# Score matmuls of two batches in four quarter tiles and two PSUM banks, with larger strided groups

## The chip, the cores and the metric

The kernel runs on one core of one Trainium2 chip. The metric is the device time of one execution in microseconds. It is one launch; inputs lie in DRAM and the output goes back there.

## The reference

Three blocks in a row over 4 batches of 576 positions: attention with 8 heads of 64, a gated feed-forward block with a spatial matmul over positions, and a block with sine and cosine and a second matmul over positions. The change is in the attention alone:

```python
B, H, S, D = q.shape                      # 4, 8, 576, 64
scores = scale * np.matmul(q, k.transpose(0, 1, 3, 2))
rel = pos[:, None] - pos[None, :]
mask_local = (rel >= 0) & (rel < stride)  # stride = 32, heads 0 to 3
mask_strided = (rel >= 0) & (pos[None, :] % stride == pos[:, None] % stride)  # heads 4 to 7
scores = np.where(masks, scores, -1e9)
attn = np.exp(scores - np.max(scores, axis=-1, keepdims=True))
attn = attn / (np.sum(attn, axis=-1, keepdims=True) + 1e-09)
out = np.matmul(attn, v)
```

## The kernel before

The two later blocks are the main work: for each batch `main_v`, `main_mid` (chunks named `u`, `sp`, `x`, `th` in the profile) and `main_end` (`y`, `c`), all matmuls in f16 with high and low parts. A chunk of main work takes one slot of the pool `ps_m`, three slots of two PSUM banks each (`pm(name)`). Attention of batch 0 runs first, that of batches 1 and 2 (`attention1`) and of batch 3 (`attention`, f16) runs beside the main work of the batch before. In the profile all instructions have line 107, the helper that records them, so one goes by tiles: `sc` scores, `sm` softmax, `st` its maxima and sums, `pT` transposed probabilities, `av` a PSUM bank for transposes and P·V, `xT` the attention's output, which is the next batch's main input.

Heads go in pairs `hp` (0 and 1 local, 2 and 3 strided); `j` is the head in the pair, and head `j` of a pair lies on partitions 64j to 64j + 63 of `q` and `k`, so its matmuls use row half j of the array. Because of the mask a local block of 64 queries needs 96 keys, and a strided block (queries and keys sorted by position modulo 32) 54 queries and 54 keys, of which the tile holds 64. `groups` (line 452) joins blocks to groups: five local ones of 4, 4, 2, 4, 4 blocks and four strided ones of 6, 6, 6, 4. A group is one chain: `gr_scores` (two matmuls a block, one a head, head j's queries on output partitions 64j and up, all in the one bank `sc`, with a mask added by a matmul of the identity), `gr_shift` (VectorE: maximum, subtraction), `gr_exp` (ScalarE), `gr_div` (VectorE: sum, two small ones, product), `gr_turn` (TensorE transposes into `av`, ScalarE copy to `pT`), `gr_px` (P·V: `v` stationary, `pT` moving, head j on output partitions 64j and up; local groups into `av`, strided ones with alternate blocks in `sc` and `av`) and `gr_parts` (ScalarE and VectorE write high and low part of `xT`). `sc` and `av` are one bank each with a single buffer.

`attention1` is a generator: step s emits P·V of group s - 2, scores, maximum, subtraction and exponential of group s, the transposes of s - 1 and the division of s, and gives control back. `others`, called after each piece of main work, takes the next step of batch b when the main matmuls' own clock has reached `ATT_AT[b][0] + n * ATT_AT[b][1]` us (line 57). That is the order in which instructions are handed over. A planner then orders each engine's instructions by its own estimate of when each is ready, gives out the slots of the pools as they come free in that estimate, and sets the semaphores; `not_before` keeps scores behind a main matmul 3 us of the clock earlier. On the chip each engine runs its instructions in the order planned. So a matmul that has to wait holds up all of TensorE behind it.

Of the kernel before, what the change touches and what calls it, by code (L numbers as in the profile page):

```python
# [56 lines left out]
ATT_AT = (None, (2.7, 3.9), (86.0, 5.0), (174.5, 4.6))  # L57
# [12 lines left out]
def kernel(  # L70
# [397 lines left out]
    def load_vl(b, hp, v):  # L468
        src = vl_d[b, hp].rearrange("p n j d -> p n (j d)")
        c = slice(1, VW - 1)  # L470
# [7 lines left out]
    def load_vs(b, v, hps=(2, 3)):  # L478

        src = vs_d[b].rearrange("h p n j d -> p h n (j d)")  # L480
        c = slice(1, VW - 1)
# [3 lines left out]
        for i in range(11):  # L485
            k, end = CB * i, min(CB * i + CB, S)
            o = 0
            while k < end:
# [6 lines left out]
                else:  # L495
                    for u, hp in enumerate(hps):
                        r = 64 * (hp - 2) + o
                        nc.sync.dma_start(v[r:r + m, u, i // 2, c], src[p0:p0 + m, hp - 2, n])
# [3 lines left out]
    mask64 = const.tile([P, 2, 96], BF16, name="mask64")  # L502
    mask54 = const.tile([P, QB], BF16, name="mask54")

    def make_masks():
# [14 lines left out]
        for j in range(2):  # L520
            h = slice(64 * j, 64 * j + 64)
            nc.vector.tensor_copy(mask64[h], a[h, j])
# [57 lines left out]
    def gr_div(g, sm, st):  # L580

        local, blocks = groups[g]
        n, w = len(blocks), 96 if local else QB
        p, sums = sm[:, 0:n * w].rearrange("p (n c) -> p n c", c=w), st[:, 1, 0:n]
        nc.vector.tensor_reduce(out=sums, in_=p, op=ALU.add, axis=mybir.AxisListType.X)
        nc.vector.tensor_scalar(sums, sums, 1e-9, 1.0 / XS, op0=ALU.add, op1=ALU.mult)
        nc.vector.reciprocal(sums, sums)
        nc.vector.tensor_tensor(p, p, sums.unsqueeze(2).broadcast_to([P, n, w]), ALU.mult)

# [35 lines left out]

    def gr_px(b, g, v, pT):


        local, blocks = groups[g]
        banks = (pa("av"),) if local else (pa("sc"), pa("av"))  # L630
        nb = len(banks)
        for i, (hp, blk) in enumerate(blocks):
            r = 64 * (i % 2)
            m = QB if local else min(CB, S - CB * blk)
            for j in range(2):
                c = slice(1 + 64 * j, 65 + 64 * j)
                q = slice(64 * j, 64 * j + m)
                if local:
                    lhs, rhs = v[hp][0:96, blk, c], pT[0:96, i, q]
                else:  # L640
                    lhs, rhs = v[hp][r:r + m, blk // 2, c], pT[r:r + m, i // 2, q]
                nc.tensor.matmul(banks[i % nb][64 * j:64 * j + 64, QB * (i // nb):QB * (i // nb) + m], lhs, rhs,
                                 start=True, stop=True)
        for i in range(nb):
# [662 lines left out]
```

## Time and profile before

| what | value |
|---|---|
| time, median of 3 runs | 500.48 us (500.36 to 502.01) |
| the profiled execution, its span from first to last instruction | 505.4 us |
| instructions | 10756 |
| TensorE busy in the span | 482.8 us |
| VectorE, ScalarE, GpSimd busy | 303.1, 268.1, 73.5 us |
| mean granted clock of TensorE | 0.985 of full speed |

The profiled execution is one of its own, and its span is the time that the profile gives for it. Busy times of an engine are unions: overlapping matmuls count once. In a timeline row the first number is the start, the second the time from the first start to the last end of the instructions merged in the row; in brackets stands the idle time before it and what ended it.

### The profile page before, as it was taken

To read this page: it belongs to the slowest core of one execution; us is meant where nothing else is said; L and a number is where in the kernel's file an instruction comes from. 1 tells how busy PE (TensorE), PEld (TensorE's weight loads), DVE (VectorE), ACT (ScalarE), POOL (GpSimd) and SP (SyncE) were. 2 spreads that over 40 slices of the span, in tenths; PEclk is the share of its full clock that TensorE was granted. 3 is DMA by queue.
4 is the path that set the end of the run, shared out by engine and by line. 5 is a ranking of instruction groups with operands and counts; after the bars stand their busy time and mean duration, and the time that the engine had idled before them with its cause. 6 is when DMAs were issued, how large, how long until landed. Compare 5 with 4: busy or idle time off the path is not lost. (4 is left out here: it accounts for less than half of the span.)

```text
span 505.4 us, 10756 instructions
## 1 busy us (share of the span) xinstructions
PE 482.8 (96%) x4420; PEld 361.0 (71%) x4420; DVE 303.1 (60%) x649; ACT 268.1 (53%) x484; POOL 73.5 (15%) x69
## 2 busy tenths in 40 slices
PE   7789988999899999999999999899999999999997
PEld 5575666766467777777748878677757777777775
DVE  3665899676798545763398678773498121217412
ACT  2555877778975234445684657765772022148302
POOL 2022324320003300021000510021003200210220
PEclk9969999999899999999999999999999999999999
DMA  7967456684671036200076054521090020002602
GB/s 181 266 205 187 143 182 197 251 249 119 167 185 39 1 119 197 73 27 3 2 163 177 17 126 128 120 53 22 7 173 10 0 94 1 1 2 66 122 1 95
DMA packets 71820, 52.72 MB, mean 104 GB/s; under 512 B 50584, under 2 KB 59992, under 8 KB 71770
## 3 DMA queue, kind: packets, MB, share of 16 engines
q1 hardware_dynamic: 71466, 51.42, 37.7%
q8 instruction: 35, 0.57, 0.5%
q10 hardware_dynamic: 304, 0.61, 0.4%
q14 instruction: 15, 0.12, 0.1%
HBM read 35.36 MB, written 4.72 MB: 79 GB/s over the span
## 5 line engine op out<-in xcount | busy, mean ns | idle before, releaser
L107 PE MATMUL y<-wtok,zf 128*128 128x288 f16 x864 | 107.4, 286 | 0.4 <-DMA zf<-vn 0.4
L107 PEld LDWEIGHTS <-zf 128*128 128x128 f16 x864 | 84.1, 98 | 22.9 <-issue 1.2
L107 PE MATMUL th<-x2h,wth 128*128 128x288 f16 x384 | 50.4, 292 | 2.3 <-DVE ta L107 2.3
L107 PE MATMUL sp<-wsp,vn 128*128 128x288 f16 x384 | 51.0, 286 | 0.6 <-POOL vn L107 0.6
L107 PE MATMUL u<-xT,win 128*128 128x288 f16 x384 | 50.0, 286 | 0.0
L107 PE MATMUL x<-zf,wout 128*128 128x288 f16 x384 | 49.6, 286 | 0.0
L107 PE MATMUL v<-win,xT 128*128 128x512 f16 (+1 forms) x240 | 48.3, 380 | 1.1 <-DVE xT L107 1.1
L107 PEld LDWEIGHTS <-vn 128*128 128x128 f16 x416 | 40.2, 98 | 10.8 <-POOL vn L107 0.9
L107 POOL TENSOR_TENSOR x2h<-x2f,x2h 128x576 f16<-128x576 f32 x19 | 26.2, 1383 | 144.5 <-issue 80.2
L107 PEld LDWEIGHTS <-wth 128*128 128x128 f16 x384 | 37.9, 100 | 12.9 <-DVE ta L107 2.6
L107 PE MATMUL c<-x2h,wch 128*128 128x288 f16 x360 | 45.4, 286 | 0.0
L107 PEld LDWEIGHTS <-wch 128*128 128x128 f16 x384 | 37.4, 98 | 9.2
L107 PEld LDWEIGHTS <-win 128*128 128x128 f16 x384 | 37.3, 98 | 9.2
L107 PEld LDWEIGHTS <-wout 128*128 128x128 f16 x384 | 36.7, 98 | 9.5
L107 PEld LDWEIGHTS <-xT 128*128 128x128 f16 (+1 forms) x240 | 21.0, 100 | 25.8 <-issue 2.8
L107 ACT ACTIVATE x2h<-x2f 128x576 f16<-128x576 f32 (+1 forms) x28 | 20.9, 747 | 26.8 <-DVE x2f L107 25.4
L107 DVE SCALAR_TENSOR_TENSOR x2f<-y,x2f 128x576 f32<-128x576 f32 x16 | 12.1, 755 | 28.0 <-PE y L107 27.9
L107 DVE TENSOR_TENSOR ta<-ta,x2f 128x1152 f32<-128x1152 f32 (+1 forms) x17 | 21.6, 1283 | 10.3 <-ACT ta L107 10.3
L107 POOL TENSOR_TENSOR zf<-u,zf 128x576 f16<-128x576 f32 x8 | 10.2, 1280 | 119.6 <-ACT zf L107 78.2
L107 DVE TENSOR_TENSOR u<-u,sp 128x576 f32<-128x576 f32 x16 | 12.0, 751 | 25.1 <-PE sp L107 25.1
L107 ACT ACTIVATE o<-c 128x576 f32<-128x576 f32 x15 | 9.6, 643 | 31.8 <-PE c L107 31.6
L107 DVE SCALAR_TENSOR_TENSOR o<-x2f,o 128x576 f32<-128x576 f32 (+1 forms) x17 | 12.2, 721 | 22.3 <-ACT o L107 22.3
(142 smaller groups left out, 749.4 us busy)
## 6 DMA issues: line engine op xcount, KB each, us to landing
out_dram<-o SPq DMA_DIRECT2D x15, 288.0 KB
kt<-in_qp_dram SPq DMA_DIRECT2D x8, 288.0 KB
qs<-in_qd_dram SPq DMA_DIRECT2D x8, 288.0 KB
x2f<-in_w_in_dram SPq DMA_DIRECT2D x2, 1024.0 KB
zf<-in_w_in_dram SPq DMA_DIRECT2D x2, 1024.0 KB
xT<-in_w_ch_dram SPq DMA_DIRECT2D x2, 1024.0 KB
kt<-in_kzl_dram SPq DMA_DIRECT2D x8, 152.0 KB
ks<-in_kl_dram SPq DMA_DIRECT2D x4, 304.0 KB
```

Source lines behind the costliest of these rows:

```text
L107: ins = f(*args, **kwargs)
```

## The change

For batches 1 and 2 the groups become `quads` of slots, and a slot holds two query blocks. In the scores the two blocks of a slot go to the two partition halves of the output, and each head has a PSUM bank of its own, so the four matmuls of a slot use the four quarters of the array. The two banks are a slot of `ps_m`, the main work's pool, in place of `sc`. Local groups keep their blocks (4, 4, 2, 4, 4); strided groups hold 8, 6 and 8 blocks in place of 6, 6, 6, 4. Mask matmuls stand behind the scores, one or two for each head, except in the group with the short last blocks, where they stand first. The maximum, the subtraction and the exponential run over both banks in one instruction each. Local P·V goes to `sc`; strided P·V goes to `sc` or `av` by the block's parity. The v tiles have 128 columns in place of 130. The steps of `attention1` come 4.2 and 5.4 us of the clock apart in place of 3.9 and 5.0. Batch 0 and batch 3 stay as they are, but for a third mask made at the start.

```diff
@@ -54,7 +54,7 @@
 E_ZLO = 'vvvvvvvv'
 WARM = 6
 LEAD = 3.0
-ATT_AT = (None, (2.7, 3.9), (86.0, 5.0), (174.5, 4.6))
+ATT_AT = (None, (2.7, 4.2), (86.0, 5.4), (174.5, 4.6))
 PREP_AT = (112.0, 126.0, 131.0)
 CONV_SP = (20.0, 9.9, 1.9)
 CONV_OUT = (37.0, 12.0, 5.0)
@@ -467,7 +467,7 @@
 
     def load_vl(b, hp, v):
         src = vl_d[b, hp].rearrange("p n j d -> p n (j d)")
-        c = slice(1, VW - 1)
+        c = slice(1, VW - 1) if b == 0 else slice(0, P)
         if b == 0:
             nc.gpsimd.memset(v[:, 0:9, 0:VW:VW - 1], 1.0)
         nc.sync.dma_start(v[0:96, 0:9:3, c], src[0:96, 0:6:2])
@@ -478,7 +478,7 @@
     def load_vs(b, v, hps=(2, 3)):
 
         src = vs_d[b].rearrange("h p n j d -> p h n (j d)")
-        c = slice(1, VW - 1)
+        c = slice(1, VW - 1) if b == 0 else slice(0, P)
         hs = slice(hps[0] - 2, hps[-1] - 1)
         for n in range(len(hps) if b == 0 else 0):
             nc.gpsimd.memset(v[:, n, 0:6, 0:VW:VW - 1], 1.0)
@@ -494,12 +494,12 @@
                     nc.sync.dma_start(v[r:r + m, :, i // 2, c], src[p0:p0 + m, hs, n])
                 else:
                     for u, hp in enumerate(hps):
-                        r = 64 * (hp - 2) + o
+                        r = 64 * (hp - 2) * (b == 0) + o
                         nc.sync.dma_start(v[r:r + m, u, i // 2, c], src[p0:p0 + m, hp - 2, n])
                 k += m
                 o += m
 
-    mask64 = const.tile([P, 2, 96], BF16, name="mask64")
+    mask64 = const.tile([P, 3, 96], BF16, name="mask64")
     mask54 = const.tile([P, QB], BF16, name="mask54")
 
     def make_masks():
@@ -519,7 +519,8 @@
         nc.gpsimd.memset(a[:, :, 1, 0:STRIDE], -8e9)
         for j in range(2):
             h = slice(64 * j, 64 * j + 64)
-            nc.vector.tensor_copy(mask64[h], a[h, j])
+            nc.vector.tensor_copy(mask64[h, 0:2], a[h, j])
+            nc.vector.tensor_copy(mask64[h, 2], a[h, j, 1 - j])
         keep(b, [[-64, 2], [-NCLS, 4], [-1, NCLS]], 0, 1)
         keep(b, [[64, 2], [NCLS, 4], [0, NCLS]], NCLS - 1, -1)
         for j in range(2):
@@ -576,16 +577,6 @@
     def gr_exp(g, sm):
         n = len(groups[g][1]) * (96 if groups[g][0] else QB)
         nc.scalar.activation(sm[:, 0:n], sm[:, 0:n], AF.Exp, scale=0.125)
-
-    def gr_div(g, sm, st):
...
 
     def gr_turn(g, sm, pt, pT):
         local, blocks = groups[g]
@@ -622,27 +613,6 @@
         nc.vector.tensor_tensor(xn[:, 0:m].rearrange("p i (j d) -> p i j d", j=2),
                                 pv[:, 0:m, 1:VW - 1].rearrange("p i (j d) -> p i j d", j=2),
                                 ri.unsqueeze(3).broadcast_to([P, m, 2, 64]), ALU.mult)
-
-    def gr_px(b, g, v, pT):
...
 
     def gr_out(b, g, xn, xt):
         for i in range(len(groups[g][1]) // 2):
@@ -728,6 +698,115 @@
             for f in end:
                 f()
 
+    quads = [(True, [((0, i), (0, i + 1)), ((0, i + 2), (0, i + 3))]) for i in (0, 4)]
+    quads += [(True, [((0, 8), (1, 8))])]
+    quads += [(True, [((1, i), (1, i + 1)), ((1, i + 2), (1, i + 3))]) for i in (0, 4)]
+    quads += [(False, [((hp, i), (hp, i + 2)) for i in (0, 1, 4, 5)]) for hp in (2, 3)]
+    quads.insert(6, (False, [((2, i), (3, i)) for i in (10, 8, 9)]))
+    NQ = len(quads)
+
+    def qd_size(g):
+        local, slots = quads[g]
+        return local, slots, len(slots), 96 if local else QB
+
+    def qd_scores(g, q, k, sc):
+
+        local, slots, ns, w = qd_size(g)
+        partial = any(blk == 10 for slot in slots for hp, blk in slot)
+        runs = [(0, ns, mask64[:, 0] if local else mask54)]
+        if local and slots[0][0][1] == 0:
+            runs = [(0, 1, mask64[:, 2]), (1, ns, mask64[:, 0])]
+
+        def masks():
+            for j in range(2):
+                for r0, r1, m in runs:
+                    ins = nc.tensor.matmul(sc[:, j, r0 * w:r1 * w].rearrange("p (n c) -> p n c", c=w), identb,
+                                           m.unsqueeze(1).broadcast_to([P, r1 - r0, w]),
+                                           start=(partial and r0 == 0), stop=(not partial and r1 == ns))
+                    if partial and j == r0 == 0:
+                        not_before(ins)
+
+        if partial:
+            masks()
+        for s, slot in enumerate(slots):
+            for j in range(2):
+                h = slice(64 * j, 64 * j + 64)
+                for half, (hp, blk) in enumerate(slot):
+                    o = (QB if local else CB) * blk
+                    m, c = min(QB, S - o), w if local else min(w, S - o)
+                    ins = nc.tensor.matmul(sc[64 * half:64 * half + m, j, s * w:s * w + c], q[hp][h, o:o + m],
+                                           k[hp][h, o:o + c], start=(not partial and s == 0),
+                                           stop=(partial and s == ns - 1))
+                    if not partial and s == j == half == 0:
+                        not_before(ins)
+        if not partial:
+            masks()
+
+    def qd_softmax(g, sc, sm, st):
+        local, slots, ns, w = qd_size(g)
+        n = 2 * ns
+        sv = sc[:, :, 0:ns * w].rearrange("p j (n c) -> p j n c", c=w)
+        mx = st[:, 0, 0:n].rearrange("p (j n) -> p j n", j=2)
+        nc.vector.tensor_reduce(out=mx, in_=sv, op=ALU.max, axis=mybir.AxisListType.X)
+        nc.vector.tensor_tensor(sm[:, 0:n * w].rearrange("p (j n c) -> p j n c", j=2, c=w), sv,
+                                mx.unsqueeze(3).broadcast_to([P, 2, ns, w]), ALU.subtract)
+        nc.scalar.activation(sm[:, 0:n * w], sm[:, 0:n * w], AF.Exp, scale=0.125)
+
+    def qd_div(g, sm, st):
+
+        local, slots, ns, w = qd_size(g)
+        n = 2 * ns
+        p, sums = sm[:, 0:n * w].rearrange("p (n c) -> p n c", c=w), st[:, 1, 0:n]
+        nc.vector.tensor_reduce(out=sums, in_=p, op=ALU.add, axis=mybir.AxisListType.X)
+        nc.vector.tensor_scalar(sums, sums, 1e-9, 1.0 / XS, op0=ALU.add, op1=ALU.mult)
+        nc.vector.reciprocal(sums, sums)
+        nc.vector.tensor_tensor(p, p, sums.unsqueeze(2).broadcast_to([P, n, w]), ALU.mult)
+
+    def qd_places(g):
+
+
+        local, slots, ns, w = qd_size(g)
+        if local:
+            return [f * w for f in range(2 * ns)], lambda j, s: (j * ns + s, 0)
+        odd = ns % 2
+        starts = []
+        for j in range(2):
+            starts += [j * ns * w] * odd + [(j * ns + s) * w for s in range(odd, ns, 2)]
+        half = len(starts) // 2
+        return starts, lambda j, s: (j * half + (s + odd) // 2, 64 * ((s + odd) % 2) if s or not odd else 0)
+
+    def qd_turn(g, sm, pt, pT):
+        local = quads[g][0]
+        w, n = (96, P)[not local], len(qd_places(g)[0])
+        for t, c in enumerate(qd_places(g)[0]):
+            nc.tensor.transpose(pt[0:w, t, :], sm[:, c:c + w], ident)
+        nc.scalar.activation(pT[0:w, 0:n], pt[0:w, 0:n], AF.Copy)
+
+    def qd_px(b, g, v, pT):
+
+
+        local, slots, ns, w = qd_size(g)
+        place = qd_places(g)[1]
+        banks = (pa("sc"),) if local else (pa("sc"), pa("av"))
+        held = [[] for _ in banks]
+        for s, slot in enumerate(slots):
+            for half, (hp, blk) in enumerate(slot):
+                e = 0 if local else blk % 2
+                m = QB if local else min(CB, S - CB * blk)
+                o = QB * len(held[e])
+                held[e].append((hp, blk))
+                for j in range(2):
+                    t, r = place(j, s)
+                    q = slice(64 * half, 64 * half + m)
+                    if local:
+                        lhs, rhs = v[hp][0:96, blk, 64 * j:64 * j + 64], pT[0:96, t, q]
+                    else:
+                        assert r == 64 * e
+                        lhs, rhs = v[hp][r:r + m, blk // 2, 64 * j:64 * j + 64], pT[r:r + m, t, q]
+                    nc.tensor.matmul(banks[e][64 * j:64 * j + 64, o:o + m], lhs, rhs, start=True, stop=True)
+        for e in range(len(banks)):
+            gr_parts(b, local, held[e], banks[e], len(banks))
+
     def attention1(b):
         q, k, v = {}, {}, {}
 
@@ -736,7 +815,7 @@
             load_qk(b, hp, q[hp], k[hp], 0, S)
 
         def load_b(hp):
-            v[hp] = att_p.tile([P, 9, VW], F32, tag="vT", name="v32", bufs=2)
+            v[hp] = att_p.tile([P, 9, P], F32, tag="vT", name="v32", bufs=2)
             if hp < 2:
                 load_vl(b, hp, v[hp])
             else:
@@ -749,32 +828,31 @@
         load_b(1)
         loads = {2: (load_a, 2), 4: (load_a, 3), 5: (load_b, 2), 6: (load_b, 3)}
         un = {}
-        for s in range(NG + 2):
+        for s in range(NQ + 2):
             def turn():
                 sm, pT, st = un[s - 1]
-                gr_turn(s - 1, sm, pa4("av"), pT)
-
-            if s == NG:
+                qd_turn(s - 1, sm, pa4("av"), pT)
+
+            if s == NQ:
                 turn()
             if s >= 2:
                 sm, pT, st = un.pop(s - 2)
-                gr_px(b, s - 2, v, pT)
-            if s < NG:
-                sm = att_p.tile([P, 384], F32, tag="sm", name="sm", bufs=2)
+                qd_px(b, s - 2, v, pT)
+            if s < NQ:
+                sm = att_p.tile([P, 512], F32, tag="sm", name="sm", bufs=2)
                 pT = att_p.tile([P, 4, P], F32, tag="pT", name="pT32", bufs=2)
-                st = att_p.tile([P, 2, 6], F32, tag="st", name="st", bufs=4)
+                st = att_p.tile([P, 2, 8], F32, tag="st", name="st", bufs=4)
                 un[s] = (sm, pT, st)
-                sc = pa("sc")
-                gr_scores(s, q, k, sc)
-                gr_shift(s, sc, sm, st)
-                gr_exp(s, sm)
+                sc = pm("a1")
+                qd_scores(s, q, k, sc)
+                qd_softmax(s, sc, sm, st)
             if s in loads:
                 f, hp = loads[s]
                 f(hp)
-            if 1 <= s < NG:
+            if 1 <= s < NQ:
                 turn()
-            if s < NG:
-                gr_div(s, *un[s][::2])
+            if s < NQ:
+                qd_div(s, *un[s][::2])
             yield
 
 
```

## Rows read from the trace of the kernel before

**Rows 1.** The page, busy time of the engines (us, share of the span, instructions).
```profile
PE 482.8 (96%) x4420; PEld 361.0 (71%) x4420; DVE 303.1 (60%) x649; ACT 268.1 (53%) x484; POOL 73.5 (15%) x69
```
**Rows 2.** Busy time by stretch: batch 1's attention, to `y`, batch 2's attention.
```profile
core 0: us, PE busy (x) PEld busy (x) DVE busy (x) ACT busy (x) POOL busy (x), PEclk, DMA share, GB/s
53.70:128.10 74.40, 66.80 (x720) 49.69 (x719) 61.31 (x126) 57.80 (x91) 18.45 (x14) 1.00 0.61 192
128.10:144.60 16.50, 16.50 (x85) 8.33 (x85) 13.57 (x16) 16.47 (x23) 0.00 (x0) 0.90 0.64 166
...
166.70:237.00 70.30, 69.93 (x777) 54.18 (x777) 40.45 (x89) 28.01 (x58) 4.90 (x4) 1.00 0.24 75
```
**Rows 3.** TensorE's waits, 50 to 145 us (total us, times, longest).
```profile
PE th L107 <- DVE ta L107: 2.3, 1, 2.3
PE av L107 <- DVE xT L107: 1.6, 2, 0.8
PE sc L107 <- DVE xT L107: 0.9, 1, 0.9
PE sc L107 <- DVE sm L107: 0.7, 1, 0.7
```
**Rows 4.** Instructions grouped by form, the score matmuls of all batches.
```profile
L107 PE MATMUL sc<-kt 64*64 64x96 f32 x160 | 9.4, 250 | 1.1 <-DVE sm L107 0.7 <-issue 0.2 <-DVE st L107 0.2
...
L107 PE MATMUL sc<-kt 64*64 64x64 f32 x160 | 6.4, 223 | 0.0
```
**Rows 5.** Timeline of TensorE: local groups of batch 1, one of batch 2.
```profile
53.69 0.88 PE L107 MATMUL sc<-kt 64*64 64x96 f32 x16
54.50 0.34 PE L107 MATMUL sc<-mask,identb 128*128 128x384 bf16 x1
54.67 0.60 PE L107 MATMUL av<-ident,sm 128*96 128x128 f32 x4
55.11 3.10 PE L107 MATMUL u<-xT,win 128*128 128x288 f16 x24
...
61.75 0.55 PE L107 MATMUL sc<-kt 64*64 64x96 f32 x8 [0.74 <-DVE sm L107]
62.23 0.26 PE L107 MATMUL sc<-mask,identb 128*128 128x192 bf16 x1
62.33 0.29 PE L107 MATMUL u<-xT,win 128*128 128x288 f16 x1
...
173.05 0.34 PE L107 MATMUL sc<-mask,identb 128*128 128x384 bf16 x1
```
**Rows 6.** Timeline of TensorE: two strided groups of batch 1.
```profile
99.75 0.92 PE L107 MATMUL sc<-kt 64*64 64x64 f32 x24
100.59 0.55 PE L107 MATMUL av<-ident,sm 128*128 128x128 f32 x3
...
113.06 0.68 PE L107 MATMUL sc<-kt 64*64 64x64 f32 x16
113.67 0.55 PE L107 MATMUL av<-ident,sm 128*128 128x128 f32 x3
```
**Rows 7.** Timeline of TensorE: first and last of 24 P·V records; 12 of another group.
```profile
96.40 0.26 PE L107 MATMUL sc<-pT,v 54*64 54x54 f32 x2
...
96.75 0.22 PE L107 MATMUL av<-pT,v 54*64 54x54 f32 x2
...
105.67 0.54 PE L107 MATMUL sc<-pT,v 54*64 54x54 f32 x12
```
**Rows 8.** Timeline of VectorE: the subtraction from `sc`, batch 1 and batch 2.
```profile
61.16 0.54 DVE L107 TENSOR_TENSOR sm<-sc,st 128x384 f32<-128x384 f32 x1
...
174.17 0.56 DVE L107 TENSOR_TENSOR sm<-sc,st 128x384 f32<-128x384 f32 x1
```
**Rows 9.** Timeline of ScalarE, 112 to 130 us.
```profile
114.25 0.49 ACT L107 ACTIVATE pT<-av 128x384 f32<-128x384 f32 x1 [2.65 <-PE av L107]
...
126.43 1.71 ACT L107 ACTIVATE ta<-th 128x576 int32<-128x576 f32 x3
```
**Rows 10.** Timeline of TensorE: the last `th` chunk of batch 0.
```profile
128.10 4.79 PE L107 MATMUL th<-x2h,wth 128*128 128x288 f16 x24 [2.25 <-DVE ta L107]
```

More of the change, by code (lines that the diff above doesn't have):

```diff
@@ L578, in gr_exp @@
         nc.scalar.activation(sm[:, 0:n], sm[:, 0:n], AF.Exp, scale=0.125)
-    def gr_div(g, sm, st):
[L582 to L588, printed above, removed]
     def gr_turn(g, sm, pt, pT):
@@ L624, in gr_pv @@
                                 ri.unsqueeze(3).broadcast_to([P, m, 2, 64]), ALU.mult)
-    def gr_px(b, g, v, pT):
[L629 to L644, printed above, removed]
-            gr_parts(b, local, blocks[i::nb], banks[i], nb)
     def gr_out(b, g, xn, xt):
```

## The prediction

> **What bounds the kernel now.** I read the engines' busy times first, because they say which engine's work is worth removing: TensorE is busy 96% of the span [rows 1]. An average over the span hides stages, so next come busy times by stage. The change lies in two stretches: batch 1's attention runs from about 54 to 124 us, batch 2's from 167 to 237 us. In the second TensorE is busy 69.93 of 70.30 us, VectorE 40.45 and ScalarE 28.01: only TensorE's own work counts there. In the first (up to 128.1 us) TensorE is busy 66.80 of 74.40 us, with VectorE at 61.31 and ScalarE at 57.80: three engines nearly full, so TensorE also waits [rows 2]. The chain of waits says for what: 2.3 us for `th`'s evacuation, 1.6 us for the `av` bank, 0.9 and 0.7 us for the `sc` bank [rows 3]. Hence an edit that shortens TensorE's work pays in full in batch 2, and in batch 1 only where the wait after it shortens too.
>
> **Scores.** Per batch there are 40 blocks (18 local, 22 strided) of two heads, so 80 fp32 matmuls; the trace has two records for each (144 of the 160 local records and 160 of the strided ones are these batches', 16 more strided ones are 36 wide) [rows 4]. The pace comes from two groups of different size: 16 local records take 0.81 us up to the next instruction, 8 take 0.48, so one costs 0.041 us and a run 0.15 us besides [rows 5]. Strided: 24 take 0.84, 16 take 0.61, so 0.029 us each and 0.15 us a run [rows 6].
>
> What would four tiles do? The P·V matmuls of the strided blocks already show it. Where both banks were free, 24 records on four tiles (two row halves, one bank each, times two column halves) last from 96.40 to 96.97 us, 0.57 us; where only one bank's 12 were issued, on two tiles, they last 0.54 us [rows 7]. So four tiles go at twice the pace of two. The new scores have exactly that layout: a head's row half writes a bank of its own, and two query blocks take the two column halves. The instruction count stays 80 a batch, the pace doubles: 144 x 0.041 / 2 = 2.95 us and 176 x 0.029 / 2 = 2.55 us, together **-5.5 us** over both batches. The bounds are 0 (they still run two at a time) and this; I take the full value, since the row it rests on is the same kind of matmul in the same tiles.
>
> **Groups.** Nine groups become eight: a run of scores and a run of P·V fewer per batch. Four runs at 0.15 us: **-0.6 us**. VectorE loses one set of its six instructions per batch. The columns it reads stay the same, and the path does not feel it in batch 2.
>
> **Masks.** 11 mask matmuls per batch become 20 over the same columns. A 384-wide one takes 0.17 us to the next instruction, a 192-wide one 0.10 [rows 5], so splitting costs at most 0.03 us; 18 more at 0.02 is **+0.3 us**. Whether they stand before or behind the scores changes nothing: either way the array goes from full tiles to quarter tiles and back once. The third mask's two small copies run on VectorE at the very start, under the first loads; I cost them at nothing, and late they would hold up the first mask matmul by their own length.
>
> **Transposes.** The strided group of six takes two for each head, so 12 a batch in place of 11; four last 0.44 us to the next instruction [rows 5], so two more are **+0.2 us**.
>
> **P·V.** The count stays, the order does not. A block's row half now goes by its parity, and a slot's two blocks share it, so four matmuls in a row sit on two tiles before the other row half's turn. From below: the tiles fill anyway, 176 records at the four-tile pace, 0.0145 us each, 2.6 us. From above: two at a time, 5.1 us. Before, 88 of the records ran four at a time and 88 two at a time (three strided groups of batch 2 and one of batch 1 were issued with both banks free), 3.8 us. The middle of the bounds is the same 3.8, so I take **0**, with -1.2 to +1.3 for the range. The Trainium skill's page "TensorE: Matmul & The Clock Gate", in "The mechanism", has matmuls start and end strictly in program order. By that rule this term would lie near its upper end and the forecast would be about 1 us later; the alternating `sc` and `av` starts [rows 7] agree with the order, and no run here shows blocks that share a row half.
>
> The sum of TensorE's own work is -5.5 - 0.6 + 0.3 + 0.2 = **-5.6 us, 2.8 a batch**.
>
> **Where the scores wait now.** They leave `sc` for a two-bank slot of the pool of three that main chunks use. So they no longer wait for P·V's evacuation or for the previous subtraction in `sc` (0.9 + 0.7 us), and local P·V moves from `av` to `sc`, so a transpose no longer waits for that evacuation (1.6 us) [rows 3]; together 3.2 us of waits in batch 1 may go. In exchange a main chunk may wait for a slot that VectorE still reads. In batch 2 the subtraction ends at 174.73 us, after a mask that ended at 173.39: 1.3 us, less than half of the 3.1 us of a main chunk (24 `u` matmuls) [rows 5, 8], so the other two slots cover it. In batch 1 one group's mask ended at 54.84 and its subtraction at 61.70, 6.9 us later [rows 5, 8]; this is the exposed place. The v tiles lose their two padding columns; the loads keep their number and 512-byte pieces and lie under other work, as they do now (no wait for `v` among the larger ones [rows 3]), so I cost them at nothing; late, they would hold up a P·V run.
>
> **What batch 1 keeps.** Its stretch ends in a wait that TensorE's speed cannot shorten: the last `th` chunk starts at 128.10 after waiting 2.25 us for the evacuation of the first, which ScalarE issued at 126.43 [rows 9, 10]. An earlier TensorE alone would only wait longer. But ScalarE itself had stood 2.65 us waiting for the last group's transposes, until 114.25 [rows 9], and those stood behind scores that waited for `sc`. With a group fewer and that wait gone, ScalarE's queue, and with it the evacuation, moves up by about 2.65 us. I take that for batch 1 and not the larger 2.8 + 3.2. The last chunk's 24 matmuls took 4.79 us where a like chunk took 3.10 [rows 5, 10], and the granted clock of the stretch is 0.90 [rows 2]: after the long wait TensorE ran for a while at its lower level (1.2 of 2.4 GHz). If the wait vanished, up to 1.7 us more would come back.
>
> **Likeliest: 495.0 us.** 2.8 (batch 2) + 2.65 (batch 1) = 5.45 off. The profiled execution lasted 505.4 us, 4.9 more than the median of 500.48 of the unprofiled runs. I take the difference from the profile as it is and set it against the median. Its own range is 492 to 497; chance 0.54.
>
> **Rivals.** *Batch 1 gives it all back*: the conversions on ScalarE keep their times, `th` still starts at 128.1, and only batch 2's 2.8 us stay: 497.7 us. For it: 61.31 and 57.80 busy us of 74.40 [rows 2]; against it: the 2.65 us of idle ScalarE [rows 9]. Chance 0.24. Beside this stands the Trainium skill's page "TensorEngine Tiling (Array Packing)", "PSUM Bottleneck": tiling speeds up the matmuls and not the emptying of PSUM, which may become the limit. By that rule batch 1 would gain nothing, which is this rival's time; the trace agrees in that VectorE is late in batch 1 [rows 8], and in batch 2 it is not. *The tiles do not double*: the scores run at their old pace and the rest cancels (-0.6 + 0.5): 500.4 us. Against it stands the P·V row [rows 7]. Chance 0.08. *The shared slots cost more than the tiles save*: in batch 1 a slot is held 6.9 us while a main chunk takes 3.1; if the sequence of slots leaves main only one other, the chunk after waits 3.8 us. One such wait leaves a gain of 1.8; from the second on the change loses: 500.5 - 5.6 + 7.6 = 502.5 us. For it: VectorE's lateness [rows 8]; against it: three slots, and two chunks already cover 6.2 of the 6.9 us. Chance 0.14.
>
> **Range and chances.** A measurement of this kernel cannot tell changes under about 0.3% (1.5 us) from none. The fast end is the likeliest with P·V at its good end (1.2), half of the 3.2 us of waits gone besides (1.6) and the clock's 1.7: 490.5. The slow end lies past the first two rivals and takes in part of the last: 501.0. Faster: nearly all of the likeliest and most of the first rival, 0.73. Same: the second rival, the slow edge of the first, one slot wait, 0.13. Slower: the last, 0.14.
>
> **What would show it.** Right: strided score runs of 32 records in about 0.6 us and local ones of 16 in about 0.5 us; no `sc` waits in batch 1; batch 2's stretch 2.8 us shorter with TensorE still near 99% busy; the first `th` evacuation 2 to 3 us earlier. Wrong: score runs at the old pace; TensorE waiting for `sm` before `u`, `sp` or `x` chunks; P·V runs of the eight-block groups well over 0.7 us; or an order of main chunks around the groups that is not today's, which I cannot work out and which would move batch 1's waits either way.

## The result and the profile after

The changed kernel takes 493.91 us (median of four runs, 493.30 to 495.05), the kernel before 500.62 us in the same comparison: a ratio of 0.9862 with a 95% interval of 0.9846 to 0.9878, 6.7 us off. The forecast was 495.0 us, its range 490.5 to 501.0.

The page of the profiled execution (493.71 us, span 491.9) shows TensorE 12.8 us less busy than [rows 1]. VectorE and ScalarE hardly differ.

```profile
PE 470.0 (96%) x4440; PEld 353.6 (72%) x4440; DVE 300.8 (61%) x639; ACT 268.4 (55%) x480; POOL 72.6 (15%) x69
```

That difference is too large for the change, so a second execution of the kernel before (499.69 us, the first experiment) serves as the measure from here on. Executions of one kernel differ by some microseconds: the first profile's span of 505.4 us lies above the median of 500.6, this second one 0.9 us under that of its round (500.55). I cut both traces where the work is the same: from the first score matmul of batch 1 to the first `y` matmul (batch 1's attention with its main work), and from there to the first `y` of the next batch (batch 2's). Busy time by stretch, first the kernel before in its second profile:

```profile
37.58:138.33 100.75, 93.37 (x889) 63.42 (x890) 80.00 (x151) 80.74 (x119) 20.73 (x16) 1.00 0.63 191
138.33:256.73 118.40, 118.22 (x1134) 88.30 (x1133) 75.59 (x148) 60.17 (x100) 12.76 (x9) 1.00 0.28 78
```

The same two stretches of the changed kernel:

```profile
36.65:136.59 99.94, 90.68 (x900) 62.25 (x900) 78.60 (x147) 80.35 (x116) 19.84 (x16) 0.97 0.65 193
136.59:251.66 115.07, 114.27 (x1145) 86.19 (x1143) 75.46 (x141) 60.96 (x99) 12.74 (x9) 1.00 0.31 80
```

Batch 2's stretch is 3.33 us shorter and TensorE still busy for 99% of it. Batch 1's is only 0.8 us shorter, though TensorE has 2.7 us less to do there, and the granted clock of that stretch (third figure from the end) fell from 1.00 to 0.97. The remaining 1.8 us lie outside: 0.9 before the first score matmul, 0.4 in batch 3, 0.5 behind it.

Where TensorE's time went, by kind. Each matmul record is charged the time to the start of the next one; of a gap over 0.33 us all but 0.123 us is called a wait. Main work has 0.66 us of batch 0's last P·V in it.

| us | batch 1 before | after | batch 2 before | after |
|---|---|---|---|---|
| scores | 7.26 | 4.01 | 6.78 | 4.02 |
| masks | 1.77 | 1.62 | 1.79 | 1.54 |
| transposes | 4.05 | 4.26 | 3.57 | 3.49 |
| P·V | 6.17 | 5.68 | 5.20 | 4.99 |
| main work | 72.33 | 74.06 | 100.60 | 100.07 |
| waits | 9.17 | 10.32 | 0.47 | 0.96 |

The score runs themselves, in TensorE's timeline of the changed kernel (answers to [rows 5, 6]):

```profile
61.80 0.56 PE L107 MATMUL a<-kt 64*64 64x96 f32 x16
62.29 0.34 PE L107 MATMUL a<-mask,identb 128*128 128x96 bf16 x4
64.37 0.42 PE L107 MATMUL sp<-wsp,vn 128*128 128x288 f16 x2 [1.73 <-ACT vn L107]
66.80 0.42 PE L107 MATMUL u<-xT,win 128*128 128x288 f16 x1 [2.02 <-DVE sm L107]
...
81.36 0.69 PE L107 MATMUL a<-kt 64*64 64x64 f32 x32
81.98 0.39 PE L107 MATMUL a<-mask,identb 128*128 128x256 bf16 x2
```

From start to start a local run of 16 takes 61.80 to 62.29, 0.49 us (0.81 before), a strided run of 32 takes 0.62 us (24 took 0.84 before). With the prediction's 0.15 us a run taken off, that is 0.021 and 0.015 us a record in place of 0.041 and 0.029: twice the pace. The rows of `sp` and `u` behind the first run are the other half of the story: TensorE now stands for 1.73 and 2.02 us with 0.42 us of work in between, the second time for `sm`, the subtraction that reads the scores' slot. The waits by cause, 50 to 145 us (answer to [rows 3]):

```profile
PE av L107 <- ACT zf L107: 2.2, 1, 2.2
PE u L107 <- DVE sm L107: 2.0, 1, 2.0
PE sp L107 <- ACT vn L107: 1.7, 1, 1.7
PE av L107 <- DVE rs L107: 1.5, 1, 1.5
```

The `sc` waits of before are gone, and so is the one for `th`'s evacuation; these four are the largest in their place. The first names ScalarE's `zf`, but the transposes that wait there read `sm`, and VectorE's product that writes it ends at 90.60 us, 0.15 us before they start. So VectorE's lateness stands behind most of the four. `th`'s 96 matmuls are one row of the timeline now (answer to [rows 10]):

```profile
112.83 12.06 PE L107 MATMUL th<-x2h,wth 128*128 128x288 f16 x96
```

What happens to the clock at the waits from 62 to 67 us is in the busy times by 2 us of the changed kernel (third figure from the end, the granted clock):

```profile
62.00:64.00 2.00, 0.64 (x20) 0.37 (x14) 1.94 (x5) 2.00 (x3) 1.21 (x2) 1.00 0.93 375
64.00:66.00 2.00, 0.42 (x2) 0.11 (x2) 2.00 (x2) 2.00 (x4) 1.67 (x1) 0.75 0.18 72
66.00:68.00 2.00, 1.20 (x5) 0.79 (x6) 2.00 (x5) 0.87 (x3) 0.00 (x0) 0.50 0.00 0
68.00:70.00 2.00, 2.00 (x10) 1.28 (x9) 2.00 (x4) 1.87 (x3) 0.00 (x0) 0.50 0.00 0
70.00:72.00 2.00, 2.00 (x11) 1.27 (x10) 1.90 (x4) 1.40 (x2) 1.55 (x2) 0.54 0.77 211
72.00:74.00 2.00, 2.00 (x19) 1.60 (x17) 0.15 (x2) 0.00 (x0) 1.05 (x1) 1.00 0.76 313
```

After the two waits TensorE is at its lower level, 1.2 of 2.4 GHz: between 68 and 72 us it is busy throughout and does 21 matmuls, in the next 2 us 19. That is where most of main work's growth from 72.33 to 74.06 us comes from.

### The profile page after: what moved, and what is told of

The parts are those of the page before. It is cut to its first block, busy times and chain, and to the rows that moved or that the text cites. A ratio compares the mean times of both kernels' runs of the same rounds, so it can differ in the third digit from the quotient of the medians.

```text
span 491.9 us, 10785 instructions
## 1 busy us (share of the span) xinstructions
PE 470.0 (96%) x4440; PEld 353.6 (72%) x4440; DVE 300.8 (61%) x639; ACT 268.4 (55%) x480; POOL 72.6 (15%) x69
## 5 line engine op out<-in xcount | busy, mean ns | idle before, releaser
L107 PE MATMUL th<-x2h,wth 128*128 128x288 f16 x384 | 47.8, 286 | 0.0
L107 PEld LDWEIGHTS <-wth 128*128 128x128 f16 x384 | 37.6, 98 | 9.6 <-issue 0.2
```

Of the source, the lines that this page charges most:

```text
L107: ins = f(*args, **kwargs)
```

## The experiments

Stretches of batch 1 and batch 2 below are cut as above. Each comes from one profiled execution; in the two profiles of the changed kernel they are 99.95 and 99.98, 115.06 and 115.06 us, in the two of the kernel before 102.48 and 100.75, 118.58 and 118.40 us.

| kernel | time, us | ratio to before (95%) | batch 1 | batch 2 |
|---|---|---|---|---|
| before, second profile | 499.69 | | 100.75 | 118.40 |
| changed | 493.91 | 0.9862 (0.9846 to 0.9878) | 99.95 | 115.06 |
| changed again | 494.12 | 0.9864 (0.9823 to 0.9905) | 99.98 | 115.06 |
| batch 1 alone | 498.34 | 0.9956 (0.9932 to 0.998) | 101.29 | 118.63 |
| batch 2 alone | 495.21 | 0.9899 (0.9867 to 0.9931) | 100.50 | 115.06 |
| heads apart, masks between | 496.65 | 0.992 (0.9893 to 0.9947) | 99.31 | 119.00 |
| head after head | 494.35 | 0.9853 (0.981 to 0.9896) | 100.23 | 115.49 |
| residue off GpSimd | 492.22 | 0.9806 (0.9763 to 0.985) | 97.63 | 115.06 |
| maximum, subtraction first | 494.27 | 0.9855 (0.9807 to 0.9902) | 100.52 | 115.06 |
| the division first too | 497.36 | 0.9891 (0.9849 to 0.9933) | 103.36 | 115.06 |
| old spacing | 491.76 | 0.9814 (0.9776 to 0.9852) | 97.48 | 115.06 |
| residue off GpSimd, 4.6 us apart | 493.57 | 0.985 (0.9808 to 0.9892) | 100.05 | 115.06 |
| residue off GpSimd, 3.9 us apart | 489.53 | 0.9774 (0.9736 to 0.9812) | 95.79 | 115.06 |

**The kernel before, a second profile.** No edit.

> The kernel before, profiled once more. The profiled execution of before spanned 505.4 us and that of after 491.9, 13.5 us apart, while the unprofiled medians are 6.7 us apart; in the trace before, the first v matmul of batch 0 starts at 37.6 us, in the one after at 31.5, ahead of anything the change touches. Theory: that start is a chance of the one execution; then this profile spans about 499 us, starts v near 32 us, and batch 1's stretch (first v of batch 0 to the first y) is longer than the 107.0 us of the first trace. Rival: the start is faster because of the change; then this profile again starts v near 37 us.

499.69 us, span 497.9. The first `v` matmul starts at 32.3 us, so the late start was that one execution's and not the change's doing. The first score matmul of batch 1 starts at 37.58 us, against 42.11 in the first profile: 4.5 of the 7.5 us between the two spans lie ahead of the change. The stretch from the first `v` to the first `y` took 106.0 us and not more than 107.0, as the theory had it. Another 1.7 us lie in batch 1: both profiles wait for the last `th` chunk, 2.25 and 2.02 us, but behind the first wait the granted clock fell to 0.50, and behind the second it stayed at 1.00.

**Each batch alone.** The generator of the other batch is that of before, with its old spacing (its v tiles without the two padding columns). The edit in words, since its code is long:

```diff
-    attention1 for batches 1 and 2: quads
+    attention1 for one of them: quads; for the other: groups
```

> The change for batch 1 alone; batch 2 keeps the kernel before's groups, scores and spacing. By the prediction's sum 2.65 us off, about 498.0 us. If batch 1 gives its gain back to the late th evacuation (the first rival): 500.6. If the traces' parts are right as they stand (1.9 us between v and y): 498.7.

> The change for batch 2 alone. By the prediction's sum 2.8 us off, 497.8 us; the traces' stretch from y of batch 0 to th of batch 1 shrank by 3.5, so 497.1 by those. If the rest of the gain (about 1.4 us in batch 3's attention after it) also hangs on batch 2: 495.7.

498.34 and 495.21 us. Batch 1 alone lies between the first and the third forecast; batch 2 alone gains 5.3 us in the medians, more than any of its forecasts. Batch 2's stretch is 115.06 us wherever batch 2 has the change's order, whatever batch 1 does: 3.3 us, safe. The other 2 us of its median lie outside that stretch. Batch 1 changed alone has a stretch of 101.29 us, no shorter than the 100.75 of before, and the same four largest waits (2.2, 2.0, 1.7, 1.5 us) as when both are changed. Its 2.2 us in the medians therefore do not show in batch 1; its profile is 1.0 us shorter ahead of the first score matmul, 0.85 in batch 3 and 0.5 at the end. Single profiles settle little here: the three with batch 1's old order have a stretch of 100.50, 100.75 and 102.48 us.

**The heads apart.** One head's scores and masks are issued, then the other's, so a full-array mask matmul stands between the two row halves and only two quarters can work at a time.

The edit, shortened:

```diff
-        for s, slot in enumerate(slots):
-            for j in range(2):
+        for j in range(2):
+            if partial: masks(j)
+            for s, slot in enumerate(slots):
...
+            if not partial: masks(j)
```

> After, with one head's scores, then its mask matmuls, then the other head's: a mask matmul takes the whole array, so the two row halves can no longer run at once and two tiles are left in place of four; 16 more changes between whole array and quarters over both batches. Theory (the four tiles carry the gain): in batch 2 the score runs take 1.3 us more a group of eight strided blocks' two heads together or less, 2.75 + 8 x 0.15 = 4.0 us more in batch 2's dense stretch, and up to the same in batch 1: 498 to 502 us. Rival (the gain comes from fewer groups, the freed banks and the order): only the 16 changes at 0.15 us, 1.2 to 2.4 us: 495 to 496.3.

496.65 us. TensorE's timeline, one strided group:

```profile
82.17 0.68 PE L107 MATMUL a<-kt 64*64 64x64 f32 x16
82.79 0.28 PE L107 MATMUL a<-mask,identb 128*128 128x256 bf16 x1
83.00 0.68 PE L107 MATMUL a<-kt 64*64 64x64 f32 x16
83.61 0.28 PE L107 MATMUL a<-mask,identb 128*128 128x256 bf16 x1
```

82.17 to 83.00 and 83.00 to 83.73, 1.56 us for what takes 0.62 + 0.23 in the changed kernel. Over a batch scores go from 4.0 to 7.7 us and masks from 1.6 to 2.4. Batch 2 shows nearly all of it (115.06 to 119.00). By the expectation's estimate 1.2 us of that are the eight more changes between whole array and quarters; the rest is the score pace, so there the pace is most of the gain. Batch 1 shows none (99.31, even less than 99.95): its waits shrink from 10.3 to 4.8 us, by more than the work grows. A TensorE with 4.5 us more to do in batch 1 arrives no later, so something else sets batch 1. The theory was right for batch 2 and wrong for batch 1, which is why the time fell between the two forecasts.

**Head after head.** The same loop order, but the masks stay behind both heads.

```diff
-        for s, slot in enumerate(slots):
-            for j in range(2):
+        for j in range(2):
+            for s, slot in enumerate(slots):
```

> The changed kernel with the score matmuls of one head issued first and then those of the other (masks still behind both): only the order of the 16 to 32 score matmuls within a run differs, and in that order the first half of a run uses two of the four 64x64 tiles of the array and the second half the other two. Theory A (a matmul starts as soon as its own tile is free, and matmuls later in the order may start beside earlier ones): the runs keep the pace of the changed kernel (0.49 us for 16 records, 0.63 us for 32), and the time is that of the changed kernel, 493.9 us within 0.7. Theory B (matmuls start strictly in program order, and only neighbours in it run together): two tiles at a time, 0.8 us for 16 records and 1.2 us for 32 as with the heads taken apart, about 5 us more score time over the two batches, of which the second batch shows all: 496 to 499 us.

494.35 us: theory A's time, but not its pace. TensorE's timeline:

```profile
80.49 0.98 PE L107 MATMUL a<-kt 64*64 64x64 f32 x32
81.40 0.39 PE L107 MATMUL a<-mask,identb 128*128 128x256 bf16 x2
```

32 records take 0.91 us, between the 0.62 of the changed kernel and twice 0.62 with the heads apart. Runs of 16 stay at 0.51. The starts of the 32 say why: pairs 58 ns apart until the fifth pair at 282 and 288 ns, then two more at 294 and 301 ns, and fours until 466 ns, then pairs again. The added pair is taken to be the second head's, for two reasons: its next step comes 107 ns later, as the first head's second step comes 107 ns after its first, and only so do both heads come to 16 records. Then the second head starts when ten of the first head's 16 have started: TensorE reaches ahead in its order for a free part of the array, but only so far. The order is the program's here; the order that the planner handed over is in no row.

**A residue off GpSimd.** In the changed kernel, 63 to 67 us, VectorE and GpSimd (timelines, one fence each):

```profile
62.96 0.72 DVE L107 TENSOR_TENSOR vn<-vr,vn 64x512 f16<-64x512 f32 x1
63.71 1.99 DVE L107 TENSOR_SCALAR st<-st 128x2 f32<-128x2 f32 x1
65.61 0.55 DVE L107 TENSOR_REDUCE st<-a 128x4 f32<-128x384 f32 x1
66.08 0.15 DVE L107 RECIPROCAL st<-st 128x2 f32<-128x2 f32 x1
66.19 0.56 DVE L107 TENSOR_TENSOR sm<-a,st 128x384 f32<-128x384 f32 x1
```

```profile
63.44 2.23 POOL L107 TENSOR_TENSOR vn<-vr,vn 128x1024 f16<-128x1024 f32 x1 [0.31 <-ACT vn L107]
```

A VectorE instruction on 128x2 ends at 65.70, just after GpSimd's at 65.67; the other of its kind takes 0.17 us. The maximum and the subtraction that free the score slot stand behind it, and `u` behind those (66.80).

```diff
-E_VLO = 'vgvg'
+E_VLO = 'vvvg'
```

> The changed kernel with one piece of work moved: the second low-order residue of the normalised v in the stage that batch 1's attention lies beside (128x1024) is computed by VectorE instead of GpSimd. In the changed kernel GpSimd has it from 63.44 to 65.67 us, and in that time a VectorE instruction on 128x2 elements that takes 0.17 us elsewhere takes 1.99 us; the maximum and subtraction behind it come late, and the u chunk waits 2.30 us for the score slot (to 66.80), with a slower clock behind it. Theory (VectorE is held up by GpSimd's instruction): the 128x2 instruction is back at 0.2 us, VectorE pays about 1.2 us itself, the u wait shrinks by 0.6 to 1.8 us and with it up to 2 us of slow clock: 491 to 493.5 us. Rival (the residue is in the way on either engine, or the scheduler's order around it decides): 493.5 to 495 us.

492.22 us. The small instruction takes 0.17 us again, at 63.56. But the rest went otherwise than the theory had it: the scheduler put both residues ahead of the subtraction, which now comes at 68.17, later than before, and the `u` chunk, which stands elsewhere in the order, starts at 64.74 without waiting for it. The waits sum to 10.31 us as before; what came back is the clock (busy times by 2 us):

```profile
64.00:66.00 2.00, 1.68 (x11) 0.99 (x11) 2.00 (x3) 2.00 (x5) 0.00 (x0) 1.00 0.09 35
66.00:68.00 2.00, 1.49 (x13) 1.02 (x12) 2.00 (x5) 1.39 (x3) 0.00 (x0) 1.00 0.00 0
68.00:70.00 2.00, 2.00 (x18) 1.65 (x18) 1.38 (x4) 1.99 (x4) 1.18 (x2) 1.00 0.51 123
70.00:72.00 2.00, 2.00 (x17) 1.42 (x16) 1.79 (x4) 1.26 (x2) 1.10 (x1) 1.00 0.98 401
```

Matmuls fill the time between the waits, the clock stays at 2.4 GHz, and main work is 71.95 us in place of 74.06: 2.1 of the 2.3 us that batch 1's stretch gained. This is the profile of one execution. Of the four runs two have a mean granted clock of 1.00 (491.48 and 491.30 us) and two have 0.997 and 0.993 (492.98 and 492.96 us); all four are faster than the changed kernel's fastest (493.30).

**Priority on VectorE.** The maximum and subtraction, then also the division, get priority in the scheduler. The edit of the first, shortened:

```diff
-        nc.vector.tensor_reduce(out=mx, in_=sv, op=ALU.max, ...)
-        nc.vector.tensor_tensor(sm..., sv, mx..., ALU.subtract)
+        hv.tensor_reduce(out=mx, in_=sv, op=ALU.max, ...)
+        hv.tensor_tensor(sm..., sv, mx..., ALU.subtract)
```

> The changed kernel with the maximum and the subtraction of each group given priority on VectorE, so that the two PSUM banks of scores come free sooner. Theory (batch 1 gives its gain back because the score banks are held until the subtraction, as at 62 to 67 us): the waits for the subtraction's output ahead of a main chunk go from 2.0 us to under 0.5 us in batch 1 and the clock keeps its level behind them: 491 to 493 us. Rival (the same VectorE work only comes later: the normalised v and the x tiles are late instead, and TensorE waits for those): 493.5 to 495.5 us.

> As the kernel before it in this list, and the division (sum, reciprocal, multiply) has priority too. In the changed kernel the transposes at 88.31 us wait 2.45 us because the division runs only after 1.36 + 0.75 us of other VectorE work. Theory (attention's own chain on VectorE sets batch 1's remaining waits): that wait goes below 1 us, and the time is 1 to 2 us under that of the kernel with maximum and subtraction first, 489.5 to 492 us. Rival (VectorE's queue for the main stage is as urgent: its copies to xT and its sums u are late instead): no better than the changed kernel, 493.5 to 496 us.

494.27 and 497.36 us (nine runs from 493.21 to 498.93): no gain, the first at its rival's time, the second above it. In the first the gap ahead of `u` shrinks from 2.31 to 1.34 us, and the next `sp` matmul then starts 2.57 us after `u`'s second. But the edit did not do there what it was for: the maximum starts at 66.97 us and the subtraction at 67.70, later than in the changed kernel (65.61 and 66.19), behind a `vn` residue that takes VectorE 3.11 us while GpSimd works on the other. So whether an earlier subtraction would help there was not tested. In the second the wait ahead of the last `th` chunk is back (a gap of 3.34 us) with a slower clock behind it.

**Spacing.** The changed kernel again, then with the due times of before, then without the GpSimd residue at two spacings of batch 1.

```diff
-ATT_AT = (None, (2.7, 4.2), (86.0, 5.4), (174.5, 4.6))
+ATT_AT = (None, (2.7, 3.9), (86.0, 5.0), (174.5, 4.6))
```

> The changed kernel again, as the measure for the three beside it: 493.9 us within 0.7, with the waits at 62.4 to 66.8 us and the slower clock behind them (about 64.9 to 71 us) in the same place, if they belong to the program's order and not to chance.

> The changed kernel with the old spacing of the groups (3.9 us in batch 1 and 5.0 us in batch 2 instead of 4.2 and 5.4). Theory (what is left of batch 1's waits is a matter of where a group meets the VectorE and GpSimd work of the main stage; batch 2 has slack): batch 2's stretch stays within 0.5 us of 91.43 us, batch 1's waits move and their sum changes by up to 2 us either way: 492 to 496 us. Rival (the spacing is what makes the gain: with fewer and larger groups closer together the attention chain outruns VectorE and ScalarE): both batches lose, 496 to 500 us.

> The kernel without the GpSimd residue (492.2 us), with batch 1's groups 4.6 us apart instead of 4.2. Theory (batch 1's remaining 11 us of waits are attention's own chains through VectorE and ScalarE, which a later due time for the next step would cover with main matmuls): 489.5 to 492 us. Rival (the last group then comes so late that the evacuation of th waits behind attention's work again, 2.2 to 3.3 us with a slower clock, as in the kernel before): 493 to 496 us.

> The kernel without the GpSimd residue (492.2 us), with batch 1's groups 3.9 us apart instead of 4.2. If a shorter attention in batch 1 only meets its own chain sooner: waits of batch 1 grow by 0.5 to 2 us, 492.5 to 494.5 us. If the due times hardly matter (the scheduler places by what is ready): 491.5 to 492.8 us.

The changed kernel repeats (494.12 us, waits and slow clock in the same places). The old spacing takes 491.76 us (491.02 to 492.47, against 494.05 to 494.79), a little under the theory's 492 to 496: batch 1's waits fall from 10.3 to 7.9 us and batch 2 does not change (the expectation's 91.43 us count only up to the first `th`). So the spacing edit, which the forecast did not cost, lost 2.4 us. Without the residue, 4.6 us is worse than 4.2 (493.57 against 492.22), at the rival's time but with only 0.5 us of waiting in `th`; its largest gaps, 2.7 and 3.0 us, lie elsewhere in batch 1. 3.9 us is better than either forecast (489.53). So moving the groups further apart did not cover attention's chains.

The last kernel differs from the one with the old spacing in the residue, and in batch 2's spacing, which does not show in batch 2's stretch (115.06 us in both). It is the cleanest test of the GpSimd instruction. Old spacing, VectorE, GpSimd and TensorE in turn:

```profile
64.35 3.15 DVE L107 TENSOR_TENSOR vn<-vr,vn 128x1024 f16<-128x1024 f32 x1
```

```profile
64.29 2.13 POOL L107 TENSOR_TENSOR vn<-vr,vn 128x1024 f16<-128x1024 f32 x1 [1.26 <-ACT vn L107]
```

```profile
65.05 0.40 PE L107 MATMUL a<-mask,identb 128*128 128x192 bf16 x2
67.56 1.86 PE L107 MATMUL sp<-wsp,vn 128*128 128x288 f16 x7 [2.11 <-DVE vn L107]
```

Both residues on VectorE, the same place:

```profile
64.54 2.35 DVE L107 TENSOR_TENSOR vn<-vr,vn 128x1024 f16<-128x1024 f32 x2
```

```profile
65.24 0.34 PE L107 MATMUL a<-mask,identb 128*128 128x192 bf16 x2
65.81 3.48 PE L107 MATMUL sp<-wsp,vn 128*128 128x288 f16 x15 [0.23 <-DVE vn L107]
```

With GpSimd at work one residue takes VectorE 3.15 us; without it two take 2.35. TensorE's wait for `vn` goes from 2.11 to 0.23 us, and the time from 491.76 to 489.53, the fastest kernel here. The clock is not the reason this time, main work being 74.2 and 74.0 us. It falls here too, to 0.54 and 0.61 in the slices from 66 to 70 us, although the waits ahead of it (gaps of 1.33, 0.80 and 0.48 us) are shorter in total than those of the kernel with the residue off GpSimd and 4.2 us (1.93, 0.40 and 0.79), where it stayed at 1.00.

## Why the prediction was right, and where it was not

The time was right (1.1 us off) and so were the sign and the place of the gain in batch 2. In batch 1 the mechanism was not right, and that the total came out so close is in part luck.

- **Scores** (-5.5 us, -5.8 with the two score runs saved): right. Measured -3.25 and -2.76, -6.0 with these runs; the heads apart give it back where TensorE is the bound.
- **Masks** (+0.3): wrong in sign, -0.4. Splitting cost next to nothing (two of 192 columns 0.175 us, one of 384 0.173), and the strided groups' masks, with three groups in place of four, took 0.73 us in batch 2 in place of 1.00.
- **Transposes** (+0.2): +0.1.
- **P·V** (0, bounds -1.2 and +1.3): -0.7. TensorE's timeline of an eight-block group, first and last rows of 32 records and what follows:

```profile
94.01 0.27 PE L107 MATMUL sc<-pT,v 54*64 54x54 f32 x2
94.03 0.26 PE L107 MATMUL av<-pT,v 54*64 54x54 f32 x2
...
94.51 0.22 PE L107 MATMUL av<-pT,v 54*64 54x54 f32 x1
94.52 0.69 PE L107 MATMUL a<-kt 64*64 64x64 f32 x31
```

  0.51 us for 32 records, four at a time; at 0.029 us each, the two-tile pace, it would be 0.9. Batch 2's first such group takes 0.51 us too and its last 0.66. Batch 1's last one shows the prediction's sign of being wrong, 1.22 us, with the `av` records alone for the first 0.61:

```profile
108.66 0.67 PE L107 MATMUL av<-pT,v 54*64 54x54 f32 x14
109.27 0.50 PE L107 MATMUL sc<-pT,v 54*64 54x54 f32 x10
```

  In the program's order four `sc` matmuls stand ahead of the first `av` one; in the group at 94.01 us they alternate by twos in time. The Trainium skill's page "TensorE: Matmul & The Clock Gate", "The mechanism", has matmuls start strictly in program order; here and in the kernel with head after head they did not, unless the planner changed the order, which no row shows.
- **Batch 2 keeps 2.8**: right in mechanism; it kept 3.33, the sum of the terms above (-3.3), main work interrupted less (-0.5) and 0.5 of new waits. VectorE cost nothing else there.
- **Batch 1 keeps 2.65**: this is the step that failed. It let ScalarE's queue, and with it the first evacuation of `th`, move up by the 2.65 us that ScalarE had waited. That wait is gone, but the evacuation came only 0.7 us earlier: 83.5 us after the first scores, 84.3 before; the prediction's own sign of being right was 2 to 3 us. ScalarE in the changed kernel, then ScalarE and TensorE in the second profile of the kernel before:

```profile
120.18 1.17 ACT L107 ACTIVATE ta<-th 128x576 int32<-128x576 f32 x2
```

```profile
121.85 1.71 ACT L107 ACTIVATE ta<-th 128x576 int32<-128x576 f32 x3
123.51 1.77 PE L107 MATMUL th<-x2h,wth 128*128 128x288 f16 x13 [2.02 <-DVE ta L107]
```

  The wait ahead of the last `th` chunk vanished for another reason: `th` itself began 3.9 us later (76.2 us after the first scores, 72.2 before). Ahead of it stood 3.6 us more of waits, 2.0 more of main work, and 1.7 of attention's last runs that had lain within `th`, less 3.4 saved on scores and masks. Then it ran from 112.83 us to the next chunk at 124.72 without a stop, 11.89 us for its 96 matmuls, where the same stretch had taken 16.65 with 2.5 us of waits and 2.0 of attention within it. Net 0.8 against the second profile; against the three profiles with batch 1's old order 0.5 to 2.5; and in batch 1 alone nothing. What sets batch 1 as a whole stays open; of its waits only the ones at the GpSimd residue were traced to a cause by a run.
- **The rivals.** "Batch 1 gives it all back" is nearest to what batch 1 did: the conversions kept their times but for 0.7 us, as it said, though `th` started later and ran through. By the Trainium skill's page "TensorEngine Tiling (Array Packing)", "PSUM Bottleneck", tiling speeds up the matmuls and not the emptying of PSUM, which may become the limit. Batch 1 agrees in part: one of its new waits, `u` for `sm` with 2.02 us, is for the emptying of the scores' banks; the others are for `vn`, for the division or for `pT`. "The shared slots cost more" is right in its place and has one wait, not two: that same one, in batch 1 alone; it is also one of the prediction's signs of being wrong. "The tiles do not double" is wrong.
- **Why the total held all the same.** The changed kernel's profile is 6.0 us shorter than the second one of the kernel before: 0.8 in batch 1 and 3.3 in batch 2, and 1.8 outside. Ahead of the first scores the changed kernels reach them at 36.2 to 36.9 us, the three profiles with batch 1's old order at 37.6, 37.7 and 42.1; 0.2 us of that is a wait of the first scores that the change removes. At the end both profiles of before have a wait for a transposing DMA, 0.37 us in the second, and none of the others has it. What the change has to do with that, and with batch 3's 0.4, was not tested and stays open.
- **What was left out.** The spacing of the groups in line 57 is part of the change and had no term. It cost 2.4 us. Without it the same change takes 491.76 us, 3.2 under the forecast: the cost that was left out made up for gains that were counted too low, and this is the luck in the 1.1 us.

## What to carry to other kernels

Take what a faster stage saves only where its engine is the bound, and cut the trace into stretches that begin and end at the same work before comparing; here one stretch kept all of it and the other little. Where three engines were nearly full here, most of a saving on one of them went into its next waits, and what moved the time was where pieces fell against each other: a GpSimd instruction beside VectorE, due times 0.3 us apart. Such due times are to be tried again after each change, in both directions.

## What the runs showed of the hardware

- Matmuls for different quarters of the array start out of the program's order: with head after head a pair of records taken to be the second head's started 294 ns after the first, with six of the first head's 16 yet to start, and 32 records took 0.91 us, in place of 0.62 with the heads by turns. The order that the planner handed over is not in the traces.
- VectorE stands still beside some GpSimd instructions: 1.99 us for 0.17 us of work, and 3.15 us for 1.2, the first until GpSimd's 2.23 us were over, the second until 1.1 us after GpSimd's 2.13, about its own length. The Trainium skill's page "SBUF — State Buffer", "SBUF: two separate sides", has a port pair that VectorE and GpSimd share and that whichever starts first holds for its whole instruction while the other waits; these rows agree, GpSimd having started first both times (63.44 before 63.71 us, 64.29 before 64.35).
- TensorE's granted clock fell to 0.50 during the second of two waits, 1.73 and 2.02 us with 0.42 us of work in between, and stayed there from about 65 to 72 us, most of it busy time. A wait of this length did not always bring it down: the kernel before waited 2.25 us for `th` in one profile and 2.02 in the other, and the clock fell to 0.50 behind the first and stayed at 1.00 behind the second. Which waits do was not settled here.
